# Attention with a layer norm and a gated MLP on one core: the Sync queue's order in the first head

## The chip, the cores and the metric

The kernel runs on one core of a Trainium2 chip. The metric is the device time of one execution in microseconds (us). Three runs of the kernel before gave 1949.1, 1947.31 and 1947.94, a median of 1947.94. One more execution was profiled; its own time is 1949.38, and its span (first to last instruction) is 1947.6.

Names: PE is the matmul engine, DVE the vector engine, ACT the scalar engine, POOL the GpSimd engine, SP the Sync engine, which here does nothing but issue DMAs.

## What is computed

```python
xn = layernorm(x)                                   # x: 2048 x 640, bf16
q  = (xn @ wq) per head                             # 32 heads, head size 192
p  = softmax(q k^T * 192**-0.5)                     # k_cache, v_cache: 32 x 2048 x 192
s  = concat(p v) @ wo
g  = silu((silu(xn @ w1) * (xn @ w3)) @ w2)         # hidden size 1536
out = x + s * g
```

## The kernel before

**Heads, blocks, pairs.** Heads run one after the other. A head's 2048 queries are four blocks of 512 (qb = 0 to 3), its 2048 keys are eight pairs of tiles (p = 0 to 7). A step (qb, p) is: six score matmuls (line 382), one exp on ACT (line 388), and matmuls with the values (line 428) for an earlier step. During head h, `project_chunk` (line 270) computes the queries of head h+1, one block per qb, so in the steady state PE always has work. The queries come out in two halves, qA and qF, which two casts (lines 287, 288) take out of PSUM; POOL then makes copies with the halves of the partitions exchanged (qS, line 292, and qD, line 296), and DVE takes the largest absolute values (line 301). A bound on the scores (largest key value times largest query value, summed over partitions: line 340 by a reduction on POOL, or line 327 by a matmul for the very first block) stands in the exp in place of a row maximum.

**The first head is different.** Nothing is there yet when it starts. The layer norm of x, 16 tiles of 128 rows, is done while head 0 already runs:

- Tiles 0 to 7 are normalized by DVE and transposed by PE (line 225), then copied to xnT (line 226): query blocks 0 and 1.
- Tiles 8 to 15 are normalized by DVE (line 217) and transposed by DMA from SBUF to SBUF, `ln_send` (line 234, DMA in line 237), one DMA a tile: block 2 is tiles 8 to 11, block 3 is tiles 12 to 15. This text calls these eight DMAs **turns**.
- Head 0's own queries are projected block by block (line 279): block 1 at step (0, 5), block 2 at (1, 4), block 3 at (2, 4). Each needs all of its block of xnT.
- Head 1's queries are projected at (1, 1), (2, 1), (3, 1) and (3, 4) (line 285). They need xnT and a second copy with the partition halves exchanged, xnS. `swap_rows(qb)` (line 305) makes it, by two POOL DMAs of 320 KB for each block (line 308). This text calls them **swaps**.

**Keys and values.** `load_keys` (line 102) issues on SP the DMA transposes of a head's keys into KA and KB (line 110; two halves each for head 0, one DMA of 128 x 2048 for the others) and the load of the values, vt (line 114, 768 KB). `copy_keys` (line 117) copies halves of both into KC on POOL (lines 119, 120) and sets a column of ones in vt. `key_maxima` (line 310) takes the largest absolute values of the keys, in one piece of 2048 for head 0 and four pieces of 512 for the others (line 313).

**What sets the order.** SP and POOL each issue their DMAs in program order, and `pin` (`keep_in_program_order`) holds the instructions of head 0 in the order in which the program makes them. That order is written out by hand in the tables `extra_at`, `posts`, `key_at` and a few `if`s in the loop over (qb, p):

```python
posts = {
    (0, 5): ((ln_root, 8, 4), (ln_send, 8), (swap_rows, 1)),
    (0, 6): ((ln_send, 10),),
    ...
    (1, 4): ((ln_root, 12, 4), (ln_send, 12), (ln_send, 14)),
    (1, 5): ((swap_rows, 2),),
    (2, 5): ((swap_rows, 3),),
}
...
if (qb, p) == (0, 7):
    loads[1].update(load_keys(1))
```

So SP's queue in head 0 is: four turns (block 2), keys and values of head 1, four turns (block 3), keys and values of head 2. POOL issues the swap of block 1 right beside the first four turns, and that of block 2 right beside the second four.

**The first bound.** Head 0's very first block takes its maxima straight from PSUM. DVE's chain is: maxima of KA, of KB (line 313), of the two halves of ps (line 301), a product (line 319), a matmul that sums it (line 327), a copy (line 329); only then can the first exp run. `keep_busy` (line 180) issues matmuls with no use, so that PE isn't idle.

Of the kernel before, what the change touches and what calls it, by code (L numbers as in the profile page):

```python
# [10 lines left out]
ALU = mybir.AluOpType  # L11
# [19 lines left out]
def _kernel_impl(ctx, tc, A_x, A_k_cache, A_v_cache, A_wq, A_wo, B_w1, B_w3, B_w2, out):  # L31
# [67 lines left out]
                keep(nc.gpsimd.dma_start(out=wq[ROWS[t], :, c0:c1], in_=w.rearrange("(s p) d -> p s d", p=DT)))  # L99
        return dict(wq=wq)  # L100

    def load_keys(h, mid=None):
        keep = pin if h <= 2 else (lambda x: x)
        kh = A_k_cache[0, h]
        vh = A_v_cache[0, h]
        KA = kvp.tile([P, SK], BF16, tag="KA")
        KB = kvp.tile([P, SK], BF16, tag="KB")
        for K, c in ((KA, 0), (KB, DH - P)):
            for r in ((slice(0, HALF), slice(HALF, SK)) if h == 0 else (slice(0, SK),)):
                keep(nc.sync.dma_start_transpose(out=K[:, r], in_=kh[r, c:c + P]))  # L110
            if mid:
                mid.pop(0)()
        vt = kvp.tile([P, NKT, DH + 2], BF16, tag="vt")
        keep(nc.sync.dma_start(out=vt[:, :, 0:DH], in_=vh.rearrange("(t p) d -> p t d", p=P)))
        return dict(KA=KA, KB=KB, vt=vt)

    def copy_keys(L, keep=pin):
        L["KC"] = KC = kvp.tile([P, HALF], BF16, tag="KC", name="KC")
# [10 lines left out]
    with ExitStack() as actx:  # L129
# [140 lines left out]
        def project_chunk(h, qb, cast=nc.vector.tensor_copy):  # L270
            hd = heads[h]
            wq = hd["L"]["wq"]
            qA, qF, qS, qD, st = hd["qA"], hd["qF"], hd["qS"], hd["qD"], hd["st"]
            qs = slice(qb * 512, (qb + 1) * 512)
            ps = ps_st.tile([P, 1024], F32, tag="st2", name="ps")
            if h == 0:
                for t in range(2):
                    for c in range(DC):
                        pin(nc.tensor.matmul(ps[:, t * 512:(t + 1) * 512], lhsT=wq[:, t, c, :], rhs=xnT[:, c, qs],  # L279
                                             start=(c == 0), stop=(c == DC - 1)))  # L280
            else:
                for s in range(2 * DC):
                    for t in range(2):
                        xs = xnT if s % 2 == t else xnS
                        pin(nc.tensor.matmul(ps[:, t * 512:(t + 1) * 512], lhsT=wq[ROWS[t], s, :],  # L285
                                             rhs=xs[ROWS[t], s // 2, qs], start=(s == 0), stop=(s == 2 * DC - 1)))
            pin(cast(out=qA[:, qs], in_=ps[:, 0:512]))  # L287
            pin(cast(out=qF[:, qs], in_=ps[:, 512:1024]))
            first = h == 0 and qb == 0
# [3 lines left out]
            if first:  # L293
                keep(nc.scalar.copy(out=qD[:, qs], in_=qF[PGW:P, qs]))
            else:
                keep(nc.gpsimd.tensor_copy(out=qD[:, qs], in_=qF[PGW:P, qs]))

            def maxima():
                for col, src, r0 in ((2, ps[:, 0:512] if first else qA[:, qs], 0),
                                     (3, ps[:, 512:1024] if first else qF[:, qs], PGW)):  # L300
                    pin(nc.vector.tensor_reduce(out=st[r0:P, col, qb:qb + 1], in_=src[r0:P, :], axis=AX.X, op=ALU.max,  # L301
                                                apply_absolute_value=True))
            return maxima
# [6 lines left out]
        def key_maxima(h, s, k=0, n=1):  # L310
            c0, c1 = k * SK // n, (k + 1) * SK // n
            src, r0 = ((heads[h]["L"]["KA"], 0), (heads[h]["L"]["KB"], PGW))[s]
            pin(nc.vector.tensor_reduce(out=heads[h]["st"][r0:P, s, k:k + 1], in_=src[r0:P, c0:c1], axis=AX.X, op=ALU.max,  # L313
                                        apply_absolute_value=True))
# [7 lines left out]

        def first_bound(pr):
            hd = heads[0]
            bp = ps_o.tile([P, 2, 512], F32, tag="ob0", name="bp")
# [45 lines left out]
        def scores(hd, qb, p, fill=(0, 0, 0)):  # L371
            KA, KB, KC = hd["L"]["KA"], hd["L"]["KB"], hd["L"]["KC"]
            qs = slice(qb * 512, (qb + 1) * 512)
            lo, hi = slice(p * P, (p + 1) * P), slice(HALF + p * P, HALF + (p + 1) * P)
            st2 = ps_st.tile([P, 1024], F32, tag="st2", name="st2")
            steps = (((KA, lo, hd["qA"]), (KA, hi, hd["qA"])),
                     ((KB, lo, hd["qS"]), (KC, lo, hd["qS"])),
                     ((KC, lo, hd["qD"]), (KB, hi, hd["qF"])))
            for s, step in enumerate(steps):
                keep_busy(fill[s])  # L380
                for t, (k, ks, q) in enumerate(step):
                    pin(nc.tensor.matmul(st2[:, t * 512:(t + 1) * 512], lhsT=k[ROWS[t], ks], rhs=q[ROWS[t], qs],  # L382
                                         start=(s == 0), stop=(s == 2)))
            return st2
# [66 lines left out]
                late.pop(0)()  # L451

        start_head(0)
        for k in range(2):
            key_maxima(0, k)
        maxima = project_chunk(0, 0, nc.scalar.copy)
        maxima()
        loads[1] = load_weights(1)
        swap_rows(0)
        pr = first_product()  # L460
        early = [scores(heads[0], 0, 0, (2, 3, 0))]
        first_bound(pr)
        early.append(scores(heads[0], 0, 1))
        keep_busy(2)
# [1 line left out]
        pin(nc.gpsimd.partition_all_reduce(warm[:], heads[0]["nb"][0][:], P, bass_isa.ReduceOp.add))  # L466

        all_keys = [(s, k, NQB) for k in range(NQB) for s in range(2)]
        key_slots = list(all_keys)

        def first_project(h, qb):
            if h == 1 and qb == 0:
# [8 lines left out]
        def steps(*fs):  # L481
# [5 lines left out]
            (0, 2): ((ln_stats, 7),),  # L487
            (0, 3): ((ln_root, 6), (ln_scale, 6), (ln_stats, 8)),
            (0, 4): ((ln_stats, 9), (ln_stats, 10), (ln_stats, 11)),
            (0, 5): ((ln_root, 8, 4), (ln_send, 8), (swap_rows, 1)),  # L490
            (0, 6): ((ln_send, 10),),
            (1, 2): ((ln_stats, 12), (ln_stats, 13)),
            (1, 3): ((ln_stats, 14), (ln_stats, 15)),
            (1, 4): ((ln_root, 12, 4), (ln_send, 12), (ln_send, 14)),
            (1, 5): ((swap_rows, 2),),
            (2, 5): ((swap_rows, 3),),
        }
        extra_at = {
            (0, 3): ((next_turn, 4),),
# [7 lines left out]
            (3, 4): ((first_project, 1, 3),),  # L507
        }
        behind_at = ((2, 2), (2, 6), (3, 3), (3, 6))
        key_at = ((2, 2), (2, 3), (2, 5), (2, 6), (3, 2), (3, 3), (3, 4), (3, 5))  # L510
        behind = []
        for qb in range(NQB):
            for p in range(NPAIR):
                ex = extra_at.get((qb, p))
                advance(heads[0], qb, p, steps(*ex) if ex else None, early.pop(0) if early else None)
                if (qb, p) in behind_at:
                    behind.pop(0)()
                for f, *a in posts.get((qb, p), ()):
                    f(*a)
                if (qb, p) == (0, 7):  # L520
                    loads[1].update(load_keys(1))
                if (qb, p) == (2, 2):
                    copy_keys(heads[1]["L"])
                    loads[2] = {**load_weights(2), **load_keys(2)}
                if (qb, p) == (3, 5):
                    copy_keys(loads[2])
                if (qb, p) in key_at:
                    key_maxima(1, *key_slots.pop(0))
                if (qb, p) == (3, 6):
                    finish_head(1)  # L530
        lctx.close()
        fw = ctx.enter_context(tc.tile_pool(name="fw", bufs=1, side="right"))
        w1_sb = fw.tile([P, DC, FL - P], BF16, name="w1_sb")
# [331 lines left out]
```

## Time and profile before

| | value |
|---|---|
| median of three runs | 1947.94 us |
| the profiled execution: its own time / its span | 1949.38 / 1947.6 us |
| PE busy | 1933.0 us, 99% of the span |
| DVE, ACT, POOL busy | 59%, 62%, 23% |
| granted PE clock, mean | 0.999 |
| PE busy from 100 to 1500 us | 1400.00 of 1400 us |
| PE busy from 16.5 to 39.2 us | 22.27 of 22.70 us |
| PE busy from 39.2 to 56.6 us | 15.10 of 17.40 us |
| PE busy from 56.6 to 82.0 us | 22.80 of 25.40 us |

Each row of PE busy is one stretch of the span, in us from its start. PE is the engine with no idle time in the steady state, so the kernel's time is PE's work and, beside it, what PE waits at the two ends of the span. Head 0 ends at about 82 us.

### The profile page before, as it was taken

The page shows a single profiled execution, that of the slowest core. Times are in us where ns is not written, and L with a number is a line of the kernel's source. Part 1 is how long each engine was busy: PE and PEld are TensorE (multiplying, and loading weights), DVE is VectorE, ACT ScalarE, POOL GpSimd, SP SyncE. Part 2 cuts the span into 40 slices and gives each one's busy share as a digit, 9 for nine tenths or more (in the row PEclk, how much of TensorE's full clock was granted, in tenths as well). Part 3 has the DMA queues.
Part 4 walks back from the last instruction along what each step waited for, and adds up shares of the span by engine and source line. Part 5 has one row for each costly group of instructions (what it writes and reads, how often), then busy time and mean ns, then how long its engine had stood idle before and what let it go on. Part 6 is the DMA issues. An engine that isn't in the chain of part 4 may idle for free.

```text
span 1947.6 us, 60514 instructions
## 1 busy us (share of the span) xinstructions
PE 1933.0 (99%) x27239; PEld 1322.8 (68%) x27239; DVE 1139.6 (59%) x2266; ACT 1212.4 (62%) x1173; POOL 441.9 (23%) x641
## 2 busy tenths in 40 slices
PE   8999999999999999999999999999999999999998
PEld 5677666666666666666666666666666666577775
DVE  8666656566766666766666666666665655521111
ACT  6677777776767777777777777777777777210000
POOL 3422222222222222222222222222222210000000
PEclk9999999999999999999999999999999999999999
DMA  8732322232222233332323232323232103937882
GB/s 178 138 84 47 84 37 73 39 73 50 69 59 60 68 63 68 63 79 64 76 55 76 55 77 46 84 46 84 46 84 45 41 10 120 273 72 136 150 155 54
DMA packets 358331, 154.83 MB, mean 80 GB/s; under 512 B 309217, under 2 KB 351169, under 8 KB 358065
## 3 DMA queue, kind: packets, MB, share of 16 engines
q1 hardware_dynamic: 344560, 119.46, 28.1%
q0 software_dynamic: 8832, 26.55, 5.8%
q10 hardware_dynamic: 4672, 4.88, 1.0%
q8 instruction: 215, 3.52, 0.8%
q14 instruction: 52, 0.42, 0.1%
HBM read 56.23 MB, written 31.98 MB: 45 GB/s over the span
## 4 chain that ended last, share of the span: by engine, by line
PE 97%; DVE 1%; DMA 1%; SPq 0%; POOL 0%; ACT 0%; issue 0%; DVEq 0%; POOLq 0%
PE obank L428 35%; PE st L382 33%; PE ps L285 14%; PE ps_s L684 11%; PE ps_f L705 3%; PE ps_gu L555 1%; DMA xnT<-xn 0%; PE ps L580 0%; SPq L110 0%; PE ps L279 0%; DMA KB<-in_A_k_cache_dram 0%; DVE st L186 0%; ACT pT L388 0%; DVE st L301 0%; DVE st L313 0%
## 5 line engine op out<-in xcount | busy, mean ns | idle before, releaser
L388 ACT ACTIVATE pT<-st,nb 128x1024 bf16<-128x1024 f32 x1016 | 1131.3, 1114 | 445.8 <-PE st L382 443.5
L428 PEld LDWEIGHTS <-pT 64*128 64x128 bf16 x16384 | 715.4, 94 | 240.2 <-ACT pT L388 0.8
L428 PE MATMUL obank<-vt,pT 64*128 64x193 bf16 x16384 | 853.0, 243 | 0.1
L398 DVE COPY osum<-obank 128x386 f32<-128x386 f32 x256 | 142.4, 556 | 505.8 <-PE obank L428 505.8
L382 PE MATMUL st<-qA,KA 64*128 64x512 bf16 x2048 | 390.7, 376 | 0.5 <-ACT qA L287 0.2
L382 PE MATMUL st<-qD,KC 64*128 64x512 bf16 x1024 | 385.0, 376 | 0.0
L382 PE MATMUL st<-qS,KB 64*128 64x512 bf16 x1024 | 385.0, 376 | 0.0
L382 PE MATMUL st<-qF,KB 64*128 64x512 bf16 x1024 | 385.0, 376 | 0.0
L382 PE MATMUL st<-qS,KC 64*128 64x512 bf16 x1024 | 385.0, 376 | 0.0
L292 POOL COPY qS<-qA 64x512 bf16<-64x512 bf16 x256 | 193.4, 755 | 597.0 <-DVE qA L287 576.3
L285 PE MATMUL ps<-xnT,wq 64*128 64x512 bf16 x1240 | 288.3, 376 | 0.4 <-ACT pT L388 0.4
L285 PE MATMUL ps<-xnS,wq 64*128 64x512 bf16 x1240 | 286.7, 376 | 0.0
L382 PEld LDWEIGHTS <-KC 64*128 64x128 bf16 x2048 | 192.5, 94 | 119.2 <-issue 0.2
L684 PE MATMUL ps_s<-wo_sb,oT 128*128 128x320 bf16 (+2 forms) x1536 | 208.8, 299 | 0.0
L382 PEld LDWEIGHTS <-KB 64*128 64x128 bf16 x2048 | 192.5, 94 | 15.2 <-issue 0.4
L285 PEld LDWEIGHTS <-wq 64*128 64x128 bf16 x2480 | 122.1, 94 | 115.3 <-issue 0.6
L684 PEld LDWEIGHTS <-oT 128*128 128x128 bf16 x1536 | 148.3, 98 | 60.5
L405 DVE TENSOR_TENSOR ostage<-osum,rl_all 128x384 bf16<-128x384 f32 x256 | 148.7, 581 | 8.8
L399 DVE TENSOR_TENSOR osum<-osum,obank 128x386 f32<-128x386 f32 x256 | 142.6, 557 | 8.9
L689 DVE SCALAR_TENSOR_TENSOR tmp<-ps_s,g_all 128x320 f32<-128x320 f32 (+2 forms) x32 | 15.6, 488 | 176.0 <-PE ps_s L684 176.0
L382 PEld LDWEIGHTS <-KA 64*128 64x128 bf16 x2048 | 103.1, 93 | 17.4 <-issue 2.3
L99 POOL DMA_DIRECT2D wq<-in_A_wq_dram x62 | 45.5, 734 | 281.6 <-PE ps L285 269.5
(99 smaller groups left out, 1232.7 us busy)
## 6 DMA issues: line engine op xcount, KB each, us to landing
vt<-in_A_v_cache_dram SPq DMA_DIRECT2D x32, 768.0 KB, 6.2
o_scr<-ostage SPq DMA_DIRECT2D x64, 384.0 KB, 2.7
wo_sb<-in_A_wo_dram POOLq DMA_DIRECT2D x1, 7680.0 KB, 31.1
wq<-in_A_wq_dram POOLq DMA_DIRECT2D x31, 160.0 KB, 3.1
hT_scr<-hblk SPq DMA_DIRECT2D x16, 256.0 KB, 2.9
xnS<-xnT POOLq DMA_DIRECT2D x8, 320.0 KB, 6.3
xt<-in_A_x_dram POOLq DMA_DIRECT2D x16, 160.0 KB, 9.6
wq<-in_B_w_dram POOLq DMA_DIRECT2D x31, 80.0 KB, 2.6
```

The costliest lines, as they stand in the source:

```text
L99: keep(nc.gpsimd.dma_start(out=wq[ROWS[t], :, c0:c1], in_=w.rearrange("(s p) d -> p s d", p=DT)))
L285: pin(nc.tensor.matmul(ps[:, t * 512:(t + 1) * 512], lhsT=wq[ROWS[t], s, :], rhs=xs[ROWS[t], s // 2, qs], start=(s == 0), stop=(s == 2 * D ...
L292: keep(nc.gpsimd.tensor_copy(out=qS[ROWS[t], qs], in_=qA[ROWS[1 - t], qs]))
L382: pin(nc.tensor.matmul(st2[:, t * 512:(t + 1) * 512], lhsT=k[ROWS[t], ks], rhs=q[ROWS[t], qs], start=(s == 0), stop=(s == 2)))
L388: pin(nc.scalar.activation(out=pT2[:], in_=st2[:], func=ACT.Exp, scale=SCALE, bias=nb[:]))
L398: pin(nc.vector.tensor_copy(out=osum[:], in_=ov[:, 0, :, 0:DH + 1]))
L399: pin(nc.vector.tensor_tensor(out=osum[:], in0=osum[:], in1=ov[:, 1, :, 0:DH + 1], op=ALU.add))
L405: pin(nc.vector.tensor_tensor(out=ostage[:, b * 2:b * 2 + 2, hg * DH:(hg + 1) * DH], in0=osum[:, :, 0:DH], in1=rl.unsqueeze(2).to_broadcas ...
L428: pin(nc.tensor.matmul(acc["o"][b][:, r, (j % 2) * 256:(j % 2) * 256 + DH + 1], lhsT=pT2[ROWS[r], t * 512 + j * P:t * 512 + (j + 1) * P], ...
L555: pin(nc.tensor.matmul(ps[:, o:o + 512], lhsT=w_sb[:, c, (fl - 1) * P:fl * P], rhs=xnT[:, c, qs], start=(c == 0), stop=(c == DC - 1)))
L684: pin(nc.tensor.matmul(ps, lhsT=oT[:, k, :], rhs=wo_sb[:, k, c0:c1], start=(k == 0), stop=(k == OC - 1)))
L705: pin(nc.tensor.matmul(ps[:, pi * 512:pi * 512 + c1 - c0], lhsT=lhs[fc], rhs=w2_sb[:, fc, c0:c1], start=(fc == 0), stop=(fc == FC - 1)))
```

## The change

It reorders the issues of head 0 and changes its first bound. Nothing after head 1's first steps is touched; the work is the same but for one small DVE operation more, one key reduction cut in two, and two fewer useless matmuls.

1. `swap_rows(1)` moves from (0, 5) to (1, 2), `swap_rows(2)` from (1, 5) to (2, 2), `swap_rows(3)` from (2, 5) to (2, 3).
2. `load_keys(1)`, in one piece at (0, 7) before, is now KA at (1, 3), and KB and the values at (1, 5). With the turns at their old places, SP's queue is now: turns of block 2, KA of head 1, turns of block 3, KB and vt of head 1, then head 2's keys and values, whose call moves from (2, 2) to (2, 5).
3. The first bound: KB's maxima are taken in two halves of 1024 (the first needs only the first half of KB), put together by one more DVE operation. The second half of the first projection goes to a PSUM bank of its own (tile `bp`), so that the cast of the first half waits for the first five matmuls alone. The two useless matmuls ahead of the first scores go.
4. At the end of head 0, the bound of head 1 (`finish_head(1)`) is issued in front of head 2's key copies; before, the copies stood in front. Head 1's key copies move from (2, 2) to (2, 7), and its key maxima are taken KA first, then KB.

```diff
+    def load_keys(h, mid=None, hold=False):
...
+        def rest():
+            load(KB, DH - P)
+            keep(nc.sync.dma_start(out=vt[:, :, 0:DH], in_=vh.rearrange("(t p) d -> p t d", p=P)))
+
+        load(KA, 0)
+        if not hold:
+            rest()
+        return dict(KA=KA, KB=KB, vt=vt, rest=rest)
...
+            halves = [ps[:, 0:512], ps[:, 512:1024]]
             if h == 0:
+                if qb == 0:
+                    acc["bp"] = ps_o.tile([P, 2, 512], F32, tag="ob0", name="bp")
+                    halves[1] = acc["bp"][:, 1, :]
...
         start_head(0)
+        key_maxima(0, 0)
         for k in range(2):
-            key_maxima(0, k)
-        maxima = project_chunk(0, 0, nc.scalar.copy)
-        maxima()
+            key_maxima(0, 1, k, 2)
+        kb = heads[0]["st"][:, 1, 0:2]
+        pin(nc.vector.tensor_tensor(out=kb[:, 0:1], in0=kb[:, 0:1], in1=kb[:, 1:2], op=ALU.max))
+        project_chunk(0, 0, nc.scalar.copy)()
...
-        early = [scores(heads[0], 0, 0, (2, 3, 0))]
+        early = [scores(heads[0], 0, 0, (0, 3, 0))]
...
-        key_slots = list(all_keys)
+        key_slots = sorted(all_keys)
...
-            (0, 5): ((ln_root, 8, 4), (ln_send, 8), (swap_rows, 1)),
+            (0, 5): ((ln_root, 8, 4), (ln_send, 8)),
...
-            (1, 2): ((ln_stats, 12), (ln_stats, 13)),
+            (1, 2): ((ln_stats, 12), (ln_stats, 13), (swap_rows, 1)),
...
-            (1, 5): ((swap_rows, 2),),
-            (2, 5): ((swap_rows, 3),),
+            (2, 2): ((swap_rows, 2),),
+            (2, 3): ((swap_rows, 3),),
...
-        key_at = ((2, 2), (2, 3), (2, 5), (2, 6), (3, 2), (3, 3), (3, 4), (3, 5))
+        key_at = ((2, 2), (2, 3), (2, 6), (2, 7), (3, 2), (3, 3), (3, 4), (3, 5))
...
-                if (qb, p) == (0, 7):
-                    loads[1].update(load_keys(1))
-                if (qb, p) == (2, 2):
+                if (qb, p) == (1, 3):
+                    heads[1]["L"].update(load_keys(1, hold=True))
+                if (qb, p) == (1, 5):
+                    heads[1]["L"]["rest"]()
+                if (qb, p) == (2, 5):
+                    loads[2] = {**load_weights(2), **load_keys(2)}
+                if (qb, p) == (2, 7):
                     copy_keys(heads[1]["L"])
-                    loads[2] = {**load_weights(2), **load_keys(2)}
-                if (qb, p) == (3, 5):
-                    copy_keys(loads[2])
...
                 if (qb, p) == (3, 6):
                     finish_head(1)
+                    copy_keys(loads[2])
```

More of the change, by code (lines that the diff above doesn't have):

```diff
@@ L100, in load_weights @@
         return dict(wq=wq)
-    def load_keys(h, mid=None):
+    def load_keys(h, mid=None, hold=False):
         keep = pin if h <= 2 else (lambda x: x)
@@ L107, in load_keys, with load @@
         KB = kvp.tile([P, SK], BF16, tag="KB")
-        for K, c in ((KA, 0), (KB, DH - P)):
+        vt = kvp.tile([P, NKT, DH + 2], BF16, tag="vt")
+        def load(K, c):
             for r in ((slice(0, HALF), slice(HALF, SK)) if h == 0 else (slice(0, SK),)):
@@ L112, in load_keys @@
                 mid.pop(0)()
-        vt = kvp.tile([P, NKT, DH + 2], BF16, tag="vt")
-        keep(nc.sync.dma_start(out=vt[:, :, 0:DH], in_=vh.rearrange("(t p) d -> p t d", p=P)))
-        return dict(KA=KA, KB=KB, vt=vt)
+        def rest():
[5 more added lines that the diff above has]
+        return dict(KA=KA, KB=KB, vt=vt, rest=rest)
     def copy_keys(L, keep=pin):
@@ L275, in project_chunk @@
             ps = ps_st.tile([P, 1024], F32, tag="st2", name="ps")
+            halves = [ps[:, 0:512], ps[:, 512:1024]]
             if h == 0:
+                if qb == 0:
+                    acc["bp"] = ps_o.tile([P, 2, 512], F32, tag="ob0", name="bp")
+                    halves[1] = acc["bp"][:, 1, :]
                 for t in range(2):
                     for c in range(DC):
-                        pin(nc.tensor.matmul(ps[:, t * 512:(t + 1) * 512], lhsT=wq[:, t, c, :], rhs=xnT[:, c, qs],
-                                             start=(c == 0), stop=(c == DC - 1)))
+                        pin(nc.tensor.matmul(halves[t], lhsT=wq[:, t, c, :], rhs=xnT[:, c, qs], start=(c == 0), stop=(c == DC - 1)))
             else:
@@ L284, in project_chunk @@
                         xs = xnT if s % 2 == t else xnS
[L285 to L289, printed above, removed]
+                        pin(nc.tensor.matmul(halves[t], lhsT=wq[ROWS[t], s, :], rhs=xs[ROWS[t], s // 2, qs],
+                                             start=(s == 0), stop=(s == 2 * DC - 1)))
+            pin(cast(out=qA[:, qs], in_=halves[0]))
+            pin(cast(out=qF[:, qs], in_=halves[1]))
             keep = pin if h == 0 or h == 1 else (lambda x: x)
@@ L292, in project_chunk @@
                 keep(nc.gpsimd.tensor_copy(out=qS[ROWS[t], qs], in_=qA[ROWS[1 - t], qs]))
[L293 to L296, printed above, removed]
+            first = h == 0 and qb == 0
+            copy = nc.scalar.copy if first else nc.gpsimd.tensor_copy
+            keep(copy(out=qD[:, qs], in_=qF[PGW:P, qs]))
             def maxima():
-                for col, src, r0 in ((2, ps[:, 0:512] if first else qA[:, qs], 0),
-                                     (3, ps[:, 512:1024] if first else qF[:, qs], PGW)):
+                for col, src, r0 in ((2, halves[0] if first else qA[:, qs], 0), (3, halves[1] if first else qF[:, qs], PGW)):
                     pin(nc.vector.tensor_reduce(out=st[r0:P, col, qb:qb + 1], in_=src[r0:P, :], axis=AX.X, op=ALU.max,
@@ L324, in first_bound @@
             hd = heads[0]
-            bp = ps_o.tile([P, 2, 512], F32, tag="ob0", name="bp")
+            bp = acc["bp"]
             for t in range(2):
```

## The prediction

> **What bounds the kernel now.** First the engines' share and the table by stretches: PE is busy 1933.0 of 1947.6 us, and from 100 to 1500 us without a gap. So nothing can be won there by moving issues, and all that this change can win is what PE waits in the first 100 us. The second view is who PE waited for, 0 to 100 us (columns: us in total, times, longest):
>
> ```profile
> PE ps L279 <- DMA xnT<-xn: 5.0, 2, 2.7
> PE fill L180 <- DVE cols L145: 1.6, 1, 1.6
> PE ps L279 <- ACT xnT L226: 0.7, 1, 0.7
> PE ps L285 <- ACT pT L388: 0.4, 1, 0.4
> ```
>
> Two waits for the turns (DMA transposes of x, line 237) make 5.0 us; 0.4 stands at the start of head 1. The third view is PE's timeline at these two places (start, us, ..., idle before, releaser):
>
> ```profile
> 38.57 0.57 PE L428 MATMUL obank<-vt,pT 64*128 64x193 bf16 x8
> 41.44 0.38 PE L279 MATMUL ps<-xnT,wq 128*128 128x512 bf16 x1 [2.30 <-DMA xnT<-xn]
> ...
> 56.04 0.50 PE L428 MATMUL obank<-vt,pT 64*128 64x193 bf16 x8
> 59.20 0.38 PE L279 MATMUL ps<-xnT,wq 128*128 128x512 bf16 x1 [2.66 <-DMA xnT<-xn]
> ```
>
> PE is done at 39.14 and 56.54 and waits 2.30 and 2.66. Why are the turns late? SP's timeline and POOL's, and the turns' own view (durations in ns, min/median/max):
>
> ```profile
> 31.22 8.35 SPq L237 DMA_TRANSPOSE xnT<-xn  x4
> 39.62 2.65 SPq L110 DMA_TRANSPOSE KA<-in_A_k_cache_dram  x1
> 42.33 2.69 SPq L110 DMA_TRANSPOSE KB<-in_A_k_cache_dram  x1
> 45.06 0.58 SPq L114 DMA_DIRECT2D vt<-in_A_v_cache_dram  x1
> 47.18 9.02 SPq L237 DMA_TRANSPOSE xnT<-xn  x4
> ...
> 31.45 1.57 POOL L308 DMA_DIRECT2D xnS<-xnT  x2
> 47.53 1.37 POOL L308 DMA_DIRECT2D xnS<-xnT  x2
> ...
> L237 SPq DMA_TRANSPOSE xnT<-xn x8: 1244/2362/2559, 31.2 to 53.7; - x8
> DMA to landing us min/median/max: 3.6/6.3/8.7
> ```
>
> Each group of four turns starts within 0.4 us of a swap (line 308) on POOL. The first turn of a group takes SP about 1.25 us, the others up to 2.56. The DMA view for 33.5 to 35.0 us says what went through meanwhile:
>
> ```profile
> q0 software_dynamic: 70, 0.28, 96.9%
> q1 hardware_dynamic: 32, 0.00, 1.2%
> ```
>
> POOL's queue (q0, the swap) held 96.9% of the sixteen engines, and the turns (q1) moved next to nothing. The second group also stands behind keys and values still in flight: vt, issued at 45.06, takes 5.6 us or more to land.
>
> **Part by part.**
>
> *The first turns without the swap beside them.* DVE normalizes tile 8 at the same place, so the issues start at 31.22, less what the start wins (0.5, below): 30.7. At 1.3 us for each issue (the row's minimum of 1.24 and a gap) the last is issued at 34.6, and lands 3.6 later (the row's minimum), at 38.2. PE needs it at 39.14 - 0.5 = 38.6. So the wait of 2.30 goes. At the old pace (last issue 37.60 - 0.5, landing 3.6 later, 40.7) it keeps 2.1. I take the fast end, because all slow issues had a swap in flight and the two halves of KB at 6.84 and 8.46, each with more data than a turn, took 1.58 and 1.29 back to back with no POOL traffic; but the margin is only 0.4, so I count 2.1 of the 2.30.
>
> *The second turns without swap, KB and values.* PE reaches the projection of block 2 earlier by 0.5 + 2.1 = 2.6; DVE's chain behind it (casts, maxima, bound, normalizing tile 12) moves along, and the issues start at 47.18 - 2.6 = 44.6. KA of head 1 is ahead of them, issued by about 38.5 (2.65 on SP; landing 5.4 in its row, so done by 42). The swap of block 1 is issued on POOL behind the copies of (1, 1), which end at 37.94 now, so at 37.4, and lands by 46.5 at the slowest (8.4 us). Last turn issued at 48.5, landed by 52.1; need: 56.54 - 2.6 = 53.9. The wait of 2.66 goes. At the old pace (last issue 51.1) it keeps 0.8.
>
> *What is late next.* The swaps were hidden by far, and come closer to need. Block 1: landed by 46.5, needed by the projection at (2, 1), now at 50.28, then 47.7. Block 2: issued on POOL behind the copies of (2, 1), at 52.7 and 53.4; with 8.4 us landed by 61.8; needed at (3, 1), now 68.03, then 62.7. Block 3: behind it, landed by about 63, needed at 69.0. Cover 1.2, 0.9 and 6 us, so I cost the swaps at nothing; if the cover is gone, each late us is a us. KB and the values of head 1 are issued after the turns (49.8 and 52.5); their first readers are POOL's key copies at (2, 7), about 60, and head 1's first values, after 76: covered. These copies now stand on POOL behind block 3's bound and three weight issues, and end near 64.4, ahead of the next query copies at about 65.8: nothing. KC itself is read only by head 1.
>
> *The first bound.* DVE's rows for the start:
>
> ```profile
> 8.74 2.29 DVE L313 TENSOR_REDUCE st<-KA 128x1 f32<-128x2048 bf16 x1
> 12.19 2.28 DVE L313 TENSOR_REDUCE st<-KB 64x1 f32<-64x2048 bf16 x1 [1.17 <-DMA KB<-in_A_k_cache_dram]
> 14.49 1.40 DVE L301 TENSOR_REDUCE st<-ps 128x1 f32<-128x512 f32 x2
> ```
>
> Reducing 2048 takes 2.29 and 512 takes 0.69 (head 1's rows), so 1024 takes about 1.22. The first half of KB is there at 11.1 (POOL's copy of it starts then). Halves: 11.1 to 12.3 and 12.3 to 13.5; the joining operation 0.2: 13.7 in place of 14.47, so DVE wins 0.8. The first exp goes from 16.56 to 15.8 and ends at 16.9. Then the next thing is late: the first values matmul (17.73 now) also needs head 0's vt, issued at 10.42 and landing after 6.7 us (its row), at 17.1. So PE wins 0.5, between 0 (if vt or x slip) and 0.8. The two useless matmuls (0.2 each) stand before PE's wait for a cast: nothing. The separate bank lets the first cast start after five matmuls; DVE gets there at 13.7 anyhow, so nothing more.
>
> *Head 1's bound in front of the copies.* POOL's three instructions of 1.03, 1.04 and 0.17 stand ahead of the reduction (line 340) at 81.84, and ACT waits 0.95 for it. In front of them it runs at 79.5. PE's 0.40 goes; ACT is no bound there.
>
> **Sum.** 0.5 + 2.1 + 2.66 + 0.4 = 5.7 us. Against the profiled execution's own 1949.38 (span 1947.6 and 1.8 around it) that is 1943.7. That execution is 1.4 above the median of the runs shown, 1947.94, so the forecast for a median is **1942.2**.
>
> One rule bears on the rivals below. The Trainium skill, "DMA: Bandwidth & Descriptors", section "Queues, rings and completion order", says that each DMA engine takes turns between its queues packet by packet. The 70 and 32 packets of the window above agree with turns, of about 0.33 us for a swap's packet (96.9% of 16 engines for 1.5 us, over 70). By that rule a swap is never stuck behind a long queue of SP's, so the rival "late swap" below would drop out, and the sum stays as it is.
>
> **Rivals.**
> - *Turns keep their pace* (16%). What stretches them to 2.3 and more is not the swap. For it: the fourth of the first group took 1.97, from 37.60, when the swap was nearly through. Then the first wait keeps 2.1, the second group starts only 0.7 earlier, lands at 56.6 for a need of 55.8 and keeps 0.8. Gain 0.5 + 0.2 + 1.9 + 0.4 = 3.0: 1944.9.
> - *Late swap* (10%). SP now issues without a pause: turns, KB, values, keys and values of head 2. POOL's weights, issued at 15.25, in front of x rows still queued on SP's queue, took 6.8 us to land for 160 KB. If the swap of block 2 lands near 64.5, PE waits 1.8 at (3, 1): 1944.0.
> - *Starved x* (8%). The cast of qA starts about 1.1 us earlier, so POOL copies, then issues head 1's weights and the swap of block 0, earlier, while x tiles 8 to 11 are still landing. DVE reads them at about 22.6 and PE follows it with 0.2 us of slack. Price up to 1.5: 1943.7.
> - *Swaps squeezed out* (4%), the other side. POOL's queue carries swaps 2 and 3 (1.28 MB) while SP's carries head 1's KB and values and all of head 2's (3.1 MB). Block 2's swap decides alone: landing after 62.7 is a wait, after 68.4 the gain is gone. If both swaps must share from 58.5 on and get 80 GB/s, half of the 0.45 MB in 3 us that POOL's queue moved from 51 to 54, they land at 74.5: 11.8 of wait, 1954. Against it: the row above, where a swap takes nearly all from SP's queue.
>
> **The numbers.** Forecast 62% (its own range 1941.3 to 1943.4). Its lower end: the start wins 0.8 and the first wait goes whole (0.5 more), and 0.4 for the spread of runs; its upper end: the start wins nothing and the first wait keeps 0.7 more. The range on record takes in the rivals up to the turns' old pace, 1945.0. Less than 0.2% (3.9 us, about what a measurement can tell) is the case of the turns' pace: same 16%; slower 4%; faster 80%.
>
> **What would show it.** The four first turns issued in about 5 us, not 8.35; no wait of line 279 for xnT; the swaps' landing under 8.4 us; line 285 with no wait for xnS; the first exp at 15.8; head 1's first exp not waiting for POOL. I am wrong if turns of 2.3 us stand alone on the queue, or if a wait of line 285 for xnS appears.

## The result and the profile after

| | before | after |
|---|---|---|
| median of 18 runs of each | 1949.40 us | 1944.78 us |
| lowest and highest | 1946.75, 1951.09 | 1942.73, 1949.17 |
| ratio to before, 95% interval | | 0.9979 [0.9972, 0.9986] |
| the profiled execution: own time / span | 1949.38 / 1947.6 | 1946.29 / 1944.4 |
| PE busy from 16 to 100 us of the span | 78.14 us | 80.68 us |

The change is faster by 0.21%, about 4.1 us (2.7 to 5.5); the medians alone differ by 4.6. The forecast was 1942.2, a saving of 5.7: the direction is right and the size is too large. 1944.78 lies above the forecast's own range, 1941.3 to 1943.4, and under the 1945.0 up to which the wider range went.

Who PE waited for after the change, 0 to 100 us (us in total, times, longest):

```profile
PE fill L188 <- DVE cols L153: 1.6, 1, 1.6
PE obank L437 <- issue: 1.4, 1, 1.4
PE ps L296 <- DMA xnS<-xnT: 1.3, 1, 1.3
PE ps L291 <- ACT xnT L234: 0.7, 1, 0.7
PE st L391 <- ACT pT L397: 0.2, 1, 0.2
```

The 5.0 us for the turns and the 0.4 at head 1's start are gone. Two lines are new and take 2.7 back: 1.3 for a swap, and 1.4 in which the profile shows nothing that PE waited for. PE's timeline has all four places:

```profile
37.67 0.57 PE L437 MATMUL obank<-vt,pT 64*128 64x193 bf16 x8
38.17 1.04 PE L291 MATMUL ps<-xnT,wq 128*128 128x512 bf16 x3
...
52.78 0.50 PE L437 MATMUL obank<-vt,pT 64*128 64x193 bf16 x8
53.21 1.04 PE L291 MATMUL ps<-xnT,wq 128*128 128x512 bf16 x3
...
62.06 0.38 PE L296 MATMUL ps<-xnT,wq 64*128 64x512 bf16 x1
63.75 0.39 PE L296 MATMUL ps<-xnS,wq 64*128 64x512 bf16 x2 [1.31 <-DMA xnS<-xnT]
...
75.42 0.60 PE L437 MATMUL obank<-vt,pT 64*128 64x193 bf16 x7
77.44 0.57 PE L437 MATMUL obank<-vt,pT 64*128 64x193 bf16 x9 [1.42 <-issue]
```

At 38.17 and 53.21 no bracket follows: both projections of x start where the work ahead ends. SP's timeline says why, and what came in place of it:

```profile
30.32 5.20 SPq L245 DMA_TRANSPOSE xnT<-xn  x4
35.57 1.95 SPq L112 DMA_TRANSPOSE KA<-in_A_k_cache_dram  x1
43.92 6.21 SPq L245 DMA_TRANSPOSE xnT<-xn  x4
50.18 2.46 SPq L112 DMA_TRANSPOSE KB<-in_A_k_cache_dram  x1
52.70 0.57 SPq L118 DMA_DIRECT2D vt<-in_A_v_cache_dram  x1
53.31 13.85 SPq L112 DMA_TRANSPOSE KA<-in_A_k_cache_dram  x1
67.21 9.39 SPq L112 DMA_TRANSPOSE KB<-in_A_k_cache_dram  x1
```

Four turns take 5.20 us in place of 8.35, and 6.21 in place of 9.02. But from 50.18 on SP stands without a pause in DMAs of keys and values, and the first key transpose of head 2 (53.31) keeps it for 13.85 us. POOL's swaps of blocks 2 and 3 fall into just that stretch, and three of their four DMAs take longer to land (11.0, 13.8 and 14.2 us) than any swap before, where it was 4.3/6.3/8.4 us (POOL's timeline, then the view of all swaps):

```profile
36.93 1.57 POOL L317 DMA_DIRECT2D xnS<-xnT  x2
...
51.97 2.69 POOL L317 DMA_DIRECT2D xnS<-xnT  x4
```

```profile
DMA to landing us min/median/max: 5.1/8.1/14.2
```

The second DMA of block 2's swap, issued at 52.68, lands at 63.71, after 11.0 us; PE has needed it since 62.4. The DMA view for 54 to 59 us shows with whom it shared (packets, MB, share of 16 engines):

```profile
q1 hardware_dynamic: 1458, 0.52, 53.2%
q0 software_dynamic: 138, 0.49, 46.2%
```

POOL's queue (q0) has less than half. In the profile of before, from 33.5 to 35.0 us, it had 96.9%.

The wait of 1.42 comes with that crowd. PE's next instructions come by a DMA too (queue q8, one packet of 16 KB). The one that started at 72.52 took 3.44 us, to 75.96, and PE's wait begins at 76.02; the others between 55 and 85 us, of before and after, took 1.14 to 1.38, and no such wait goes with them. That PE waited for these instructions is argued from this coincidence. From 64 to 76 us the DMA moved about 95 GB/s, less than half of the 202 ahead of it, though its engines were counted busy (last column GB/s, ahead of it the share):

```profile
52.00:64.00 12.00, 10.64 (x146) 6.54 (x143) 8.67 (x17) 7.54 (x7) 9.24 (x15) 1.00 1.07 202
64.00:68.00 4.00, 4.00 (x55) 2.67 (x53) 3.73 (x8) 1.90 (x3) 1.19 (x2) 1.00 1.35 95
68.00:72.00 4.00, 4.00 (x54) 2.79 (x52) 1.89 (x4) 2.42 (x3) 0.64 (x2) 1.00 1.21 105
72.00:76.00 4.00, 4.00 (x66) 3.26 (x63) 1.88 (x6) 3.33 (x5) 2.95 (x5) 1.00 1.63 89
```

### The profile page after: what moved, and what is told of

The parts are those of the page before. It is cut to its first block, busy times and chain, and to the rows that moved or that the text cites. A ratio compares the mean times of both kernels' runs of the same rounds, so it can differ in the third digit from the quotient of the medians.

```text
span 1944.4 us, 60504 instructions
## 1 busy us (share of the span) xinstructions
PE 1932.6 (99%) x27228; PEld 1319.8 (68%) x27237; DVE 1141.6 (59%) x2268; ACT 1212.6 (62%) x1173; POOL 442.8 (23%) x641
## 4 chain that ended last, share of the span: by engine, by line
PE 98%; DVE 1%; DMA 1%; issue 0%; ACT 0%; POOL 0%; SPq 0%; POOLq 0%
PE obank L437 35%; PE st L391 34%; PE ps L296 14%; PE ps_s L697 11%; PE ps_f L718 3%; PE ps_gu L568 1%; DMA xnS<-xnT 1%; PE ps L593 0%; DVE st L322 0%; PE ps L291 0%; DMA x_all<-in_A_x_dram 0%; ACT pT L397 0%; DVE st L194 0%; DVE st L310 0%; DVE ostage L414 0%
```

## The experiments

The theory that this profile suggests, **crowding**: the new order frees the turns, as forecast, and puts the swaps of blocks 2 and 3 beside keys and values of SP's queue; there they are late, and slow everything else. Its first rival: the two swaps issued back to back are in each other's way. Medians of different chips differ, so each run is given against before on its own chip; these medians are of 5 to 11 runs. Line numbers shift by a few between the kernels.

**e1_hold.** Head 2's keys and values wait until POOL passes the copies of (3, 1).

```diff
                 if (qb, p) == (2, 5):
-                    loads[2] = {**load_weights(2), **load_keys(2)}
+                    loads[2] = load_weights(2)
+                if (qb, p) == (3, 2):
+                    loads[2].update(load_keys(2, gate=True))   # a POOL memset of one column of KA
```

> The changed kernel, but SP may issue head 2's keys and values only when POOL has passed the query copies of step (3, 1), by one memset of a column of KA. Theory A (head 2's keys and values, now issued without a pause at 53.3 us, crowd both the swap of block 2 and PE's instruction fetch): the swap of block 2 lands before 61, PE's wait of 1.3 us for xnS and its wait of 1.4 us without a releaser both go, span 1941.7 in place of 1944.4, about 5.5 to 6 us under the kernel before. Theory B (the two swaps issued back to back beside head 1's own keys and values are enough): the wait for xnS stays near 1.3. Theory C (the wait without a releaser has nothing to do with DMA traffic): that wait stays at 1.4.

Measured: 1943.83 against 1949.34, ratio 0.9974 [0.9964, 0.9984]. Both new waits are gone. The second DMA of block 2's swap lands at 58.83, 6.35 us from its issue, and the share of the queues from 54 to 59 us has turned:

```profile
q0 software_dynamic: 219, 0.77, 73.5%
q1 hardware_dynamic: 859, 0.30, 34.9%
```

In time, that is 0.95 us under the changed kernel's median, less than the intervals can tell. And the trace alone proves less than it seems to: e11, below, is the changed kernel as it stands, and there too both waits are missing and the shares look like these.

**e2_swap3_late.** The changed kernel with the swap of block 3 back at (2, 5).

```diff
-            (2, 3): ((swap_rows, 3),),
+            (2, 5): ((swap_rows, 3),),
```

> The changed kernel with the swap of block 3 back at (2, 5). Theory A (head 2's keys and values crowd): the wait for xnS at (3, 1) stays, 1 to 1.5 us, and the wait without a releaser stays; time as the changed kernel within 0.5. Theory B (two swaps back to back slow each other): the swap of block 2 lands under 8.4 us after its issue and the wait for xnS goes, 1.3 us less.

Measured: 1944.42 against 1949.34, ratio 0.9978 [0.9969, 0.9987]. Block 2's swap still needs 9.9 us (54.12 to 64.04), and head 2's first key transpose 9.08 on SP. So in this execution the swap is late without the other swap behind it, and the first rival falls (e10 and e11 add that a swap with the other right behind it can land in 5.95 and 6.75 us). PE waits only 0.2 for xnS here because PE itself came later, at 63.51 in place of 62.06: it had waited 1.4 and 0.8 us for DVE at the start. The issue wait, which the crowding theory expected to stay, is not there.

**e4_swaps_only.** The kernel before with nothing but the swaps moved (part 1 of the change).

```diff
-            (0, 5): ((ln_root, 8, 4), (ln_send, 8), (swap_rows, 1)),
+            (0, 5): ((ln_root, 8, 4), (ln_send, 8)),
-            (1, 2): ((ln_stats, 12), (ln_stats, 13)),
+            (1, 2): ((ln_stats, 12), (ln_stats, 13), (swap_rows, 1)),
-            (1, 5): ((swap_rows, 2),),
-            (2, 5): ((swap_rows, 3),),
+            (2, 2): ((swap_rows, 2),),
+            (2, 3): ((swap_rows, 3),),
```

> The kernel before with only the three swaps moved to (1, 2), (2, 2), (2, 3). If the swap beside them stretches the turns: the first four issue at 1.25 us each and PE's first wait of 2.3 for xnT goes. The second four still stand behind head 1's keys and values: if these count, the first of the four lands over 5 us after its issue and PE keeps 0.5 to 1.5 of its second wait; if only the swap counts, the second wait goes too. Gain 3 to 5 us, less a wait of about 1 us for xnS if the moved swaps come too late.

Measured: 1954.17 against 1949.34, ratio 1.0025 [1.0013, 1.0037]: **slower** by 4.8 us, where a gain was expected. The profiled execution, 1959.74, is the slowest of the ten. The first wait for turns is gone, and these stand in its place, with the table by stretches under them:

```profile
PE ps L285 <- DMA xnS<-xnT: 10.6, 2, 8.1
PE ps L279 <- ACT pT L388: 1.4, 1, 1.4
```

```profile
60.00:64.00 4.00, 4.00 (x74) 2.93 (x70) 3.78 (x8) 3.27 (x3) 3.36 (x6) 1.00 1.27 77
64.00:68.00 4.00, 2.00 (x33) 1.28 (x30) 3.83 (x8) 2.27 (x3) 0.00 (x0) 1.00 1.01 84
68.00:72.00 4.00, 3.58 (x47) 2.34 (x48) 2.13 (x5) 1.22 (x3) 0.51 (x1) 1.00 1.27 95
72.00:76.00 4.00, 2.70 (x45) 2.13 (x40) 2.73 (x5) 3.10 (x3) 1.32 (x3) 1.00 1.12 108
76.00:80.00 4.00, 0.00 (x0) 0.00 (x0) 0.00 (x0) 0.00 (x0) 0.00 (x0) 0.76 1.24 114
80.00:84.00 4.00, 1.17 (x6) 0.48 (x7) 0.00 (x0) 0.00 (x0) 0.00 (x0) 0.50 1.22 125
84.00:88.00 4.00, 4.00 (x22) 1.68 (x20) 0.10 (x1) 0.72 (x2) 0.45 (x1) 0.50 0.49 108
88.00:92.00 4.00, 4.00 (x74) 3.54 (x72) 1.78 (x6) 3.04 (x4) 3.77 (x6) 0.96 0.17 45
```

Here head 2's keys go out at 54.66 and 58.61, right beside the swap of block 2 (54.09 and 54.79), which lands at 68.38; block 3's needs 22 us. From 76 to 80 us no engine does anything, and the granted clock (the third column from the right) falls to 0.50.

The second line of the waits is the rest of the second wait for turns. The view puts it down to ACT, but ACT was done at 56.28; the last turn landed at 56.70, and PE starts the projection at 56.79, 0.09 behind it (in before it started at 59.20, 0.09 behind the landing at 59.11). So with keys and values ahead of the second turns, and no swap beside them, 1.4 us of that wait stay here, as the expectation had it (0.5 to 1.5).

**e5_bound_only.** The kernel before with the first bound alone (part 3), everything else as it was.

> The kernel before with only the first bound changed (KB's maxima in halves, the bank of its own, two useless matmuls less). As forecast: first exp 0.75 us earlier, PE 0.5 earlier at its first values matmul (bounded by head 0's values landing), both waits for xnT as in the kernel before. Against it: if the landing of head 0's values moves with each execution, up to 0.9; if PE's waits for xnT absorb the start, since the turns are late for another reason, nothing.

Measured: 1949.59 against 1949.34, ratio 1.0006 [0.9997, 1.0015]: no gain. From the start of DVE's maxima of KA to the first exp it took 7.49 us, where before took 7.82 (8.74 to 16.56) and after 7.07 (8.59 to 15.66). So the part shortens its chain by 0.3 to 0.75, and what PE won it gave back at the turns: the wait for xnT is 6.1 here, 5.0 before.

**e7_swaps_held.** e4 with head 2's keys and values held back as in e1, and head 1's bound ahead of the key copies.

> The kernel before with the swaps of blocks 1 to 3 moved as in the change, and with head 2's keys and values held back until GpSimd passes the copies of (3,1), some 12 us later. Without the hold the moved swaps alone left waits for xnS of 10.6 us and took 1954.17 us. Crowd theory (head 2's key transposes beside the swaps make the whole DMA slow): the waits for xnS fall from 10.6 to under 1.5 us, the second DMA of block 2's swap lands in under 9 us from its issue instead of 13.6, and the time falls by 6 to 10 us, to 1944 to 1948. Rival (the swaps are late because they are issued late, whatever runs beside them): the waits for xnS stay over 6 us and the time stays over 1951.

Measured: 1944.71 against 1949.42, ratio 0.9973 [0.9963, 0.9984], 8 runs from 1944.28 to 1945.14. No wait for xnS is left; the swap of block 2 lands 3.5 and 4.5 us after its issues, the quickest of all runs. The view of all swaps, in e4 and then here:

```profile
DMA to landing us min/median/max: 5.5/7.9/22.3
DMA to landing us min/median/max: 3.5/5.1/7.6
```

Against e4's ratio that is 0.5%, or 10 us. So the late places of the swaps cost no wait by themselves, and the waits for xnS in e4 come from head 2's keys and values. How much of the 10 us is the other difference, head 1's bound ahead of the key copies, no run tells. e7 has all of the gain of the full change, on SP's old order for head 1 and with the old first bound.

**e8_hold_keys.** Of head 2, the keys alone are held back; its values go out at once beside the swaps.

> The changed kernel, with head 2's keys held back until GpSimd passes the copies of (3,1), and head 2's values loaded at once, at (2,5), beside the swaps. Theory that it is the transposes that crowd the swaps: the second DMA of block 2's swap lands by 60.5 (in the run that held keys and values it was 58.83, in the changed kernel 63.71), no wait for xnS over 0.3 us, and no issue wait of TensorE near 76. Rival (any transfer of SyncE's queue beside the swaps does it, by its bytes): the swap lands at 62 or later and a wait for xnS of 0.5 us or more stays. The time is 1943 to 1945 by the first and 1944 to 1946 by the second.

Measured: 1943.96 against 1949.42, ratio 0.9972 [0.9960, 0.9984]. The swap lands at 63.12, 10.2 us from its issue, with a wait for xnS of 0.5; from 54 to 59 us POOL's queue had 44.4%. So in this execution plain values hold the swap up as transposes did in the changed kernel's: the rival named there holds, as far as one execution tells (in e10 and e11 the swap lands in 5.95 and 6.75 us with transposes beside it). The issue wait near 76 is gone, and the stretch from 64 to 68 moved 196 GB/s.

**e3_swaps_old.** The changed kernel with the swaps at their places of before: the new order of SP alone, with the rest.

> The changed kernel with the swaps of blocks 1 to 3 back at their places of before; the new order of SyncE's queue stays. Theory that the moved swaps free the turns: the first turns' wait of some 2 us for xnT comes back (turns issued at over 1.6 us each beside swap 1), and the swap of block 2 then falls on the second turns at about 44 to 52, so that a second wait for xnT comes back too; the time is 1946 to 1949. Rival (the new queue order alone frees the turns, since no key load goes ahead of them): no wait for xnT over 0.5 us, and 1942 to 1945, because swap 3 also stands clear of head 2's keys no more than before.

Measured: 1946.77 against 1949.42, ratio 0.9985 [0.9974, 0.9995]. Half of it came as expected:

```profile
PE ps L291 <- DMA xnT<-xn: 2.8, 1, 2.8
```

The first wait is back, because swap 1 stands beside the first turns again. The second isn't, though swap 2 stands beside the second turns: with no values ahead of them they land at 58.04, and PE comes at 58.40. e4 and e7 have it the other way round, values ahead of the second turns and no swap beside them: in e4 1.4 us of the wait stay, and in e7 the last turn lands at 54.16, just as PE comes at 54.11. So the second wait had two causes. Taking the values away was enough here, by 0.4 us; taking the swap away alone was enough in one profile and not in the other.

**e9_plain_keys.** Head 2's key loads as plain copies of the same bytes.

```diff
         def load(K, c):
+            if h == 2:
+                keep(nc.sync.dma_start(out=K.rearrange("p (t d) -> p t d", d=P),
+                                       in_=kh.rearrange("(t p) d -> p t d", p=P)[:, :, c:c + P]))
+                return
```

> The changed kernel, with head 2's two key loads as plain copies of the same 512 KB in rows of 256 bytes; their transposition is left out, so head 2's scores are of wrong keys. Theory that transposes beside GpSimd's transfers are what makes the whole DMA slow: the issue of the first of them falls from 13.85 us to under 2, both land by 75 (77.15 and 80.37 in the changed kernel), the stretch from 64 to 76 moves over 170 GB/s instead of some 95 (95, 105 and 89 in its three parts), and TensorE's issue wait of 1.4 us near 76 is gone; the swap of block 2 still lands at 62 to 64, since it waits for its share behind head 1's values, as in the run with head 2's values beside it. Rival (it is the bytes and the small rows, transposed or not): the stretch stays under 130 GB/s and both land after 76. The time is 1943 to 1945 by the first and within 1 us of the changed kernel's 1944.8 by the second.

Measured: 1944.05 against 1950.04, ratio 0.9969 [0.9959, 0.9979], and 0.4 us under the changed kernel on the same chip. The stretch from 64 to 76 moved 205 GB/s, the loads landed at 70.63 and 72.99, and no issue wait is left; but they kept SP for 4.01 and 8.35 us, not under 2, and the swap landed at 63.49 with a wait of 0.7. It would speak for the transposes as the cause of the slow stretch, if the next run but one didn't show 192 GB/s there with transposes. Inconclusive.

**e10_copies_first.** The changed kernel with head 2's key copies ahead of head 1's bound again (the order half of part 4).

```diff
+                if (qb, p) == (3, 5):
+                    copy_keys(loads[2])
                 if (qb, p) == (3, 6):
                     finish_head(1)
-                    copy_keys(loads[2])
```

> The changed kernel, with head 2's key copies back ahead of head 1's bound, at (3,5). My prediction's step was worth 0.4 us, from the wait of TensorE for ACT's weights in the kernel before. Theory now: in the changed kernel head 2's keys land late (77.15 and 80.37), so the copies ahead of the bound hold GpSimd until 81.5, the bound comes at about 82 instead of 75.2, ScalarE's first exponential of head 1 waits some 2 us, and the time is 1 to 3 us over the changed kernel's: the order is worth more than 0.4 here. Rival (the bound is not needed before 82, or the copies go as early as before): a wait of at most 0.5 us, and the changed kernel's time.

Measured: 1949.46 against 1950.04, ratio 0.9998 [0.9986, 1.0009], and 5.0 us over the changed kernel on the same chip, where 1 to 3 were expected: without this one line the change gains nothing. POOL's timeline and ACT's:

```profile
76.54 1.03 POOL L127 COPY KC<-KA 64x1024 bf16<-64x1024 bf16 x1 [2.11 <-DMA KA<-in_A_k_cache_dram]
79.14 1.04 POOL L128 COPY KC<-KB 64x1024 bf16<-64x1024 bf16 x1 [1.57 <-DMA KB<-in_A_k_cache_dram]
80.12 0.17 POOL L129 MEMSET vt<- 128x16 bf16 x1
80.38 0.47 POOL L349 PARTITION_ALL_REDUCE nb<-ns  x1
```

```profile
80.88 2.12 ACT L397 ACTIVATE pT<-st,nb 128x1024 bf16<-128x1024 f32 x2 [4.57 <-POOL nb L349]
```

The copies wait for the keys, the bound waits behind the copies, ACT for the bound, and PE for ACT, 2.4 us. The measured price is twice that. The profiled execution, 1947.93, is one of the quicker ones of this kernel (1943.73 to 1955.02), and keys that land later would cost more; but no slower one was profiled, so the rest of the price is not shown. Block 2's swap landed in 5.95 us here, with the keys beside it, and the issue wait is back, with 1.3 us.

**e11_again.** The changed kernel once more, as it stands, on the chip of e9, e10 and e12.

> The changed kernel once more. If its waits come from the order of the queues and not from one execution: block 2's swap lands at 62 to 65 with a wait for xnS of 0.3 to 2 us, the first of head 2's key loads is issued for over 8 us, and the stretch from 64 to 76 moves under 130 GB/s; TensorE's issue wait near 76 comes only where an instruction fetch falls into that stretch. The time is 1944 to 1946.

Measured: 1944.46 against 1950.04, ratio 0.9973 [0.9964, 0.9982]. The time repeats, the waits don't: neither a wait for xnS nor an issue wait. The first key transpose again keeps SP for 12.32 us, but from 54 to 59 us POOL's queue had most, and the swap landed at 60.07, 6.75 us from its issue:

```profile
q0 software_dynamic: 232, 0.82, 76.7%
q1 hardware_dynamic: 1482, 0.37, 33.6%
```

That profiled execution took 1943.42, the first one 1946.29. So one profile of this kernel is one draw: the order of the queues makes the crowd, and how the engines deal it out varies. The expected rate of under 130 GB/s from 64 to 76 us isn't there either (192), but the same trace has slow stretches with their ends (64 to 76 us in 40 slices of 0.3):

```profile
GB/s 261 369 285 306 115 178 144 170 171 112 47 34 20 44 84 289 289 291 290 128 185 137 61 13 9 172 291 290 290 276 187 201 244 261 302 281 248 203 177 238
```

Until 68.5 it falls as low as 20 GB/s; from there it runs at 289 to 291. POOL's last weights landed at 68.59 and head 1's values at 68.12, and what then runs at 290 is head 2's key transposes alone. That looks as if POOL's transfers made the slow stretch, but the row goes on: from 69.7 to 71.5 it falls to 9 GB/s, with the same transposes and nothing of POOL's under way.

**e6_hold_swap2_early** and, once more beside e11_again, **e12_again.** e1 with the swap of block 2 right behind that of block 1.

```diff
-            (1, 3): ((ln_stats, 14), (ln_stats, 15)),
+            (1, 3): ((ln_stats, 14), (ln_stats, 15), (swap_rows, 2)),
-            (2, 2): ((swap_rows, 2),),
```

> The changed kernel with head 2's keys and values held back as in the held run, and with block 2's swap right behind block 1's at (1,3), where SyncE has no transfer under way before the second turns. If the swaps are hurt only by transposes beside them: both swaps of blocks 1 and 2 land before the second turns are issued at about 44 to 48, no wait for xnS or xnT over 0.7 us, and the time is within 1 us of the held run's 1943.8. Rival (two swaps back to back still hold the queue when the second turns go out): turns issued at over 1.6 us each again and a wait for xnT of 1 us or more, 1945 to 1947.

> The changed kernel with head 2's keys and values held back and block 2's swap at (1,3), once more, beside the changed kernel on the same chip. If the waits left in the changed kernel are real time, it is faster than the changed kernel by 1 to 2.5 us, at 1942.5 to 1943.5; if they are hidden later, the two agree within 0.7 us.

Measured: 1943.05 against 1949.42, ratio 0.9964 [0.9950, 0.9977], and 1943.27 against 1950.04, ratio 0.9967 [0.9955, 0.9979]. Block 2's swap lands at 47.91, 14 us ahead of its need, the second turns are not held up enough to matter (landed at 51.66, PE at 53.41), and no wait for a transfer of x is left. On the same chip (e12) that is 1.2 us under the changed kernel's 1944.46, at the low end of what was expected if the waits are real time. All 29 runs of the changed kernel have a median of 1944.67 and a spread from 1942.73 to 1949.17, all 11 of this version 1943.10 and 1942.56 to 1944.06: 1.6 us less (resampling the runs gives 0.8 to 2.2, over several chips). It is the best version here, though its interval against before still touches that of the change.

**Together.** e3 and e5, with the swaps at their old places, and e4 are left aside here. Four profiles have nothing of head 2 on SP's queue beside the swaps (e1, e6, e7, e12); none has a wait for xnS or an issue wait. Six have (after, e2, e8, e9, e10, e11): four of them wait for xnS, 0.2 to 1.3 us, and two have the issue wait; but in e10 and e11 the swap of block 2 lands as fast as in e1 (5.95 and 6.75 us against 6.35). So head 2's transfers can make the swaps late and don't always do so; what else must come together is open.

## Why the prediction was right and where it was wrong

1. *What bounds it.* Right: the gains and losses are waits of PE before 100 us, and from 100 to 1500 us PE is as busy as before. Its busy time from 16 to 100 us goes from 78.14 to 80.68, in e11 to 83.23, and to 83.47 in e6.
2. *The first turns.* Right. "5 us, not 8.35" became 5.20, at 1.22 to 1.25 an issue; they landed at 36.88 and PE came at 38.17. The rival "turns keep their pace" fell.
3. *The second turns.* Right: landed at 51.51 (forecast 52.1), needed at 53.21. e3 adds that values out of the way would have done it without moving the swap, e4 that moving the swap alone can leave 1.4 us.
4. *The swaps.* **This step failed**: "Cover 1.2, 0.9 and 6 us, so I cost the swaps at nothing." The covers were worked with 8.4 us, the longest landing of before, where the swaps of blocks 2 and 3 had SP's keys beside them only in part. In their new place the second DMA of block 2's took 11.0 us, and block 3's 13.8 and 14.2. Cover of 0.9 us can't be called cover when the landing itself depends on what else is in flight. The step also left out what the crowd does to PE's own instructions, an issue wait of 1.4. In e11 the cover held, with 6.75 us, so the step fails in some executions and not in all. The rival "late swap" (block 2 near 64.5, 1.8 us of wait) described the first profiled execution nearly to the number: 63.71 and 1.3. I had argued it away with a rule, and left it 10%. The Trainium skill, "DMA: Bandwidth & Descriptors", section "Queues, rings and completion order", says that an engine takes turns between its queues packet by packet. The rule may stand, and my conclusion doesn't follow from it: turns mean that the swap has a share, not that it has priority, and the shares measured from 54 to 59 us are 46% in after, 44% in e8 and 77% in e11. Nor do the trace's packets take turns one for one: 1458 against 138 there, and 70 against 32 in the window of the prediction, which I read as agreeing. That window, with 96.9% for POOL's queue, was 1.5 us long and beside turns; e3 has the opposite, from 64 to 68 us, where head 2's key transposes ran and POOL's queue moved no packet, though its swaps had been issued at 64.61 and 65.31.
5. *The first bound.* 0.5 was a fair size for the chain (0.3 to 0.75 measured; the first exp came at 15.66, forecast 15.8), but e5 gained nothing by it, and its waits for turns were 1.1 longer. It seems to pay nothing as long as a later wait absorbs it: the parts of the sum are not independent.
6. *Head 1's bound in front of the copies.* **Mis-sized**: 0.4 forecast, 5.0 measured. I counted only POOL's three instructions in front of the reduction, with their durations in the trace of before. The new order makes head 2's keys land at 77.15 and 80.37; in the old place the copies wait for them with the bound behind, as e10 shows.
7. *The sum.* 5.7 forecast, 4.1 measured (2.7 to 5.5). The missing 1.6 (1.1 by the medians) agrees with what e6 and e12 win over the changed kernel, 1.2 to 1.6, that is with the crowd's price. The profiles fit too: the first took 3.1 us less than that of before, and with its 2.7 of new waits that makes 5.8; e11's, without them, took 1943.42. That the median came out at 1944.78 and not 1943.7, as 1949.40 less 5.7, is that; the other 1.5 up to the forecast is the level from which it started: 1947.94 was a median of three, and 18 runs of before have 1949.40.
8. *The other side.* "Swaps squeezed out" gave 11.8 us of wait and 1954, from 80 GB/s. e4 comes near that case: 10.6 us in its profiled execution, which took 1959.74. That its median, 1954.17, meets the 1954 is luck: e4 lacks the gains that this sum had in it. The change escapes the worst of it; that head 1's values now stand on SP's queue ahead of head 2's keys, and point 6, are likely reasons, but no run separates them.

Left open: what inside the DMA makes the slow stretches. In the long ones of after and e4 a key transpose of SP's queue and transfers of POOL's queue were in flight together. But in before, from 61 to 70 us, a swap and a key transpose overlapped in part at a mean of 217 GB/s, and key transposes are slow at times with nothing of POOL's moving: 9 to 61 GB/s in e11 from 70.6 to 71.5 us, and 44 to 109 in before from 41.0 to 41.9. Also open is why the same kernel deals 46% to POOL's queue in one execution and 77% in the next.

## What to carry to other kernels

A transfer that is moved into the gap of one queue is priced by what the other queues have in flight at its new time, not by its landing in the old place; add up the bytes that must pass before it is needed. Parts of a reordering are not worth their sum: here moving the swaps alone loses 4.8 us, all but one line gains nothing, and the whole gains 4.1. An instruction that waits for a DMA must not stand in front of one that the next stage needs. A wide spread of runs is a hint that transfers collide: here e4 and e10, with long waits behind transfers, spread over 11 us, e7 over less than 1 and e6 with e12 over 1.5. So compare medians of many runs, and take a single profile as one draw. And check whom a view names as the one waited for: in e4 it named ACT, and the landing right ahead of the start was a turn's.

## What the runs showed of the hardware that I had not expected

- Issuing one DMA transpose of 128 x 2048 kept SP for 1.92 us in e1 (at 67.12, with next to nothing else under way) and 1.95 to 2.7 in the early ones of before and after, but for 13.85 us in after and 12.32 in e11, in the crowd; everything behind it on SP waited.
- Key transposes alone moved 289 to 291 GB/s in one stretch (e11, 68.5 to 69.7 us) and 9 to 61 in another (70.6 to 71.5); beside POOL's transfers the whole DMA fell to 77 to 108 GB/s over 16 us (e4, 60 to 76 us), with the engines counted as busy.
- PE's instructions come over the same DMA engines: with a fetch of 16 KB that took 3.44 us in place of 1.14 to 1.38, PE stood still for 1.42 us, which the profile calls "issue". e10 has the same, 2.88 us and 1.3; no other profile here has a fetch over 1.7 us between 40 and 92 us, or such a wait.
- In e4 PE had nothing to do from 74.7 to 82.8 us. The granted clock was 0.50 from 78.1 to 88.3, so for 5.5 us after work came back, which makes that wait cost more than its length.
